# A gated linear attention and its perceptron on one core: the first pairs of step 0 by diagonal tiles, states inside their own outputs, and a new table of places

## The chip, the cores and the metric

One core of a Trainium2 chip runs the whole program. The metric is the device time in microseconds (us). Shorter is better. The core has five engines with a queue each: TensorE (PE, matrix products into the banks of PSUM), VectorE (DVE), ScalarE (ACT), GpSimd (POOL) and SyncE (SP, which issues the DMAs). Each works through its own queue in order and waits on semaphores for the others.

## The reference

Batch 4, 8 heads, 768 positions, 48 features a head; then a perceptron of width 2048 on 3072 tokens of 384.

```python
f = 1.0 / (1.0 + np.exp(-f_logit))
for t in range(S):
    state = f[:, :, t, :, None] * state + np.einsum('bhd,bhe->bhde', k[:, :, t], v[:, :, t])
    y[:, :, t] = np.einsum('bhd,bhde->bhe', q[:, :, t], state)
...
h = x @ w_in
g = np.where(pos, h, np.where(neg, 0.0, (h + beta) ** 2 / (4.0 * beta)))
return (g @ w_out).astype(np.float32)
```

## The kernel before

The 768 positions are six steps of 128. In a step the eight heads are four pairs; the program counts pairs through (0 to 3 are step 0, 4 to 7 step 1), and treats two pairs together. A step needs for each pair: the keys and queries multiplied by running products of the gates (`gate`, two scans by VectorE and two products), scores (keys by queries), a mask that keeps the past, the sums of masked scores by values, the products of the queries with the state from before, and the new state (keys turned over, by values). Scores in two halves of 64 positions are 64x64 tiles, of which four work at once in PE's array; the state after the first half, `later`, then serves the second half. The first step before does not use these tiles: `scores` makes whole 128x128 scores, each with a mask (`masks`), and `heads` and `thirds` make the sums.

The perceptron's work is 96 units (six steps of sixteen), and in each nine wide products into `ph` (line 317, `mm_in`) and nine into `po` (line 341, `mm_out`), of 512 columns. Between these groups stand the runs of the attention's small products for the step that comes next. Where they stand is a table: `TURNS` says behind which unit the keys of two pairs are turned over, `VISITS` gives four places for each two pairs: of their scores, of their states (`states_by_parts`), of the beginning of their outputs (`begin`), and of the end of their outputs (`outputs`). `START` lists the products of step 0 ahead of unit 0, and `AFTER` those behind it. When the places of the outputs' beginning and end are alike and nothing else is there, the outputs stand `alone` and borrow banks.

The order on each engine comes from a planner (`Plan`): it starts operations by a table of costs and writes out the order that results. It fills gaps of PE at the start with products of zeros (`warm`), and it has a model of how PE gets its instructions, in blocks of 256 (`BLOCK`, `FIRST_BLOCK`, `fetched`). Costs only set the order: on the chip every operation starts when its queue and its semaphores allow.

Constants (two masks and a unit matrix, `fixed`) are loaded. The values of the first two pairs (`va`) are loaded into `sd`.

Of the kernel before, what the change touches and what calls it, by code (L numbers as in the profile page):

```python
# [49 lines left out]
SMALL_PRODUCTS = ("scores", "scores_half", "heads", "thirds", "both", "begin", "before", "before_half", "part", "states", "parts", "parts_last")  # L50
# [4 lines left out]
            rows=316, turned_rows=150, scan=1140, dve=602, small=200, sums=467, gate=600, act=575, bits=660, round=485, copy=520, turned=412, sig=538, decay=226,  # L55
# [3 lines left out]
INSTRUCTIONS = dict(scores=32, scores_half=16, heads=32, thirds=32, both=128, begin=64, before=128, before_half=64, part=64, states=64, parts=128, parts_last=64, zeros=24, turn=8)  # L59
BLOCK, FIRST_BLOCK, AHEAD, BEHIND, FETCH, OFFSET, WAITS = 256, 193, 48, 40, 3700, 9, 1.0045  # L60
# [5 lines left out]
GATHER_BEHIND, GATHER_LATER = (0, 0, 0), 6000  # L66

TURNS = {4: 5.5, 6: 9.5, 8: 19.0, 10: 22.0, 12: 27.0, 14: 33.5, 16: 44.0, 18: 52.0, 20: 59.0, 22: 69.5}
VISITS = {4: (8.0, 8.0, 10.5, 10.5), 6: (10.5, 11, 13, 13), 8: (21.0, 21.0, 24.0, 24.0), 10: (24.0, 25, 29.0, 29.0), 12: (29.0, 32, 39.0, 39.0), 14: (39.0, 40.0, 42.0, 42.0), 16: (47.0, 47.0, 53.0, 53.0), 18: (53.0, 54.0, 60.0, 60.0), 20: (68.0, 68.0, 74.0, 74.0), 22: (74.0, 74.0, 77, 77)}
HOMES = [(k + 3) % 5 for k in range(25)]  # L70
START = (("scores", 0), ("mask", 0, 0), ("mask", 0, 1), ("last", 0), ("scores", 1), ("mask", 1, 0), ("mask", 1, 1), ("last", 1),
         ("scores", 2, 0), ("last", 2, 0), ("scores", 2, 1), ("last", 2, 1), ("first", 0), ("first", 1),
         ("mask", 2, 1), ("mask", 3, 1), ("mask", 2, 0), ("mask", 3, 0), ("second", 0), ("second", 1), ("second", 2), ("second", 3))
AFTER = {1.0: (('turn', 0), ('turn', 1), ('turn', 2)), 4.0: (('states', 0), ('states', 2)), 2.0: (('turn', 3),)}
# [24 lines left out]
class Plan:  # L99
# [7 lines left out]
    def add(self, engine, cost, emit, *deps, kb=0, count=None):  # L107
# [19 lines left out]
        if engine == "PE":  # L127
            o.count = count
# [7 lines left out]
    def fetched(self, o, zeros):  # L136
# [4 lines left out]
        self.able = max([self.able] + [d.end + d.lag(o) for d in o.deps if d.engine != "PE"])  # L141
        marks = [(b - AHEAD, 0, b) for b in self.blocks(last + AHEAD, end + AHEAD)]
        marks += [(b, 1, b) for b in self.blocks(last, end)] + [(b + BEHIND, 2, b) for b in self.blocks(last - BEHIND, end - BEHIND)]
        for at, kind, b in sorted(marks):
            t += (at - last) * step
            last = at
            if kind == 0:
                self.came[b + BLOCK] = t + FETCH
            elif kind == 1:
                t = max(t, self.came.get(b, 0))  # L150
            else:
                self.came[b + BLOCK] = max(self.came.get(b + BLOCK, 0), self.able + FETCH)
        self.at = end
        return t + (end - last) * step - o.start
# [5 lines left out]
    def order(self):  # L160
        index = {o: n for n, o in enumerate(self.ops)}
        self.at, self.came, self.able, idle = OFFSET, {}, 0, 0
# [15 lines left out]
        while done < len(self.ops):  # L178
# [31 lines left out]
            if e == "PE":  # L210
                o.zeros = zeros_for(o, idle)
                o.cost = self.fetched(o, o.zeros)
                idle = t + o.cost
# [17 lines left out]
def gla_moe(ctx: ExitStack, tc: tile.TileContext, ff, kqd, f0, vv, vad, vbd, wd, fixedd, gates, values, headsd, out):  # L231
# [26 lines left out]
    y3 = const.tile([R, 2, N], F32R, name="y3")  # L258
# [116 lines left out]
    set_kq = add("POOL", 1500, lambda: nc.gpsimd.memset(kq[NP - 1], 0.0))  # L375
# [7 lines left out]

    set_consts = add("POOL", 200, constants)

# [9 lines left out]
    add("PE", "zeros", lambda: warm(12), set_zeros)  # L395
# [108 lines left out]
    ready = {}  # L504
# [5 lines left out]
    def gate(m):  # L510
# [11 lines left out]
        if m == 0:  # L522
            ready["mask"] = ready["mask_t"] = ready["ident"] = dma(fixed, fixedd, 160)
            ready["f0"] = sca(200, lambda: nc.scalar.activation(f0s[:, 0:NI * NT * B], f0s[:, 0:NI * NT * B], AF.Sigmoid), dma(f0s, f0, 36))
        for h, (b0, b1) in enumerate(steps):
# [30 lines left out]
            for name, d in (("sg", sg), ("en", en), ("km", km), ("qm", qm), ("s2", s2)):  # L556
                c[name].append(d)
        to, f0m = whole(t), f0s[:, m * B:m * B + B]
# [4 lines left out]
    va = sd[:, 0:4 * B * 64].rearrange("u (b h e) -> u b h e", b=B, h=4)  # L563
# [13 lines left out]
    def elementwise(n):  # L577
# [14 lines left out]
        if p == NP - 1:  # L592

            cols = slice(0, 2 * N + B) if i else slice(0, N)
            gone = old(n - NP, "sc", "y", "tr", "db")
            c["to"] = []
            for t, m in enumerate(ours):
                o = gates_of[m]
                d = [o["km"], o["qm"], o["pf"][0]] if i else o["km"]
                o["to"] = [move(kq[NP - 1][z + 16 * SLICE[t]:z + 16 * SLICE[t] + 16, cols], kq[t][r:r + 16, cols], 64 if i else 32, d, set_kq, gone) for r, z in ((48, 0), (112, 64))]  # L600
# [18 lines left out]

    lent = {}  # L620
# [19 lines left out]
    def kn_of(n):  # L640

        return am[n] if n in (2, 3) else kn[n % 2]

    last_keys = [kn[0], kn[1], kn[0]]
    am_of = [am[0:2], am[2:4], [am[0], act_f[0][:, 0:N].rearrange("r (b c) -> r b c", b=B)], [am[1], kn[1]]]
# [24 lines left out]
    def masks(n, h):  # L670
# [5 lines left out]
        free = {(2, 0): lambda: att[0]["ys"][0], (3, 0): lambda: att[0]["ys"][1], (3, 1): lambda: att[3]["pt"][1]}.get((n, h), lambda: None)  # L676
        o = vec("dve", lambda: nc.vector.tensor_tensor(
            out=t, in0=ps, in1=mask.rearrange("u (o t) -> u o t", o=1).broadcast_to([C, B, C]), op=ALU.mult),
            c["sc"], ready["mask"], free())
# [10 lines left out]

    TILES = ((0, 0), (1, 1), (1, 0), (0, 1))
# [39 lines left out]
    def transpose_tensor(n, at=None):  # L731
# [9 lines left out]
        c["kn"] = [sca("turned", lambda: nc.scalar.copy(kn_of(n)[:, :, :R], ps[:, :, :R]), c["tr"], old(n - 2, "st") if n > 3 else [], [att[3]["sc"], att[3]["y"]])]  # L741
# [44 lines left out]
    def outputs(n, unit, alone):  # L786
# [5 lines left out]
        def decayed(which):  # L792

            def emit():
                parts = ((0, ds[n // 2 % 2]), (1, later))[::1 if which is False else -1]
# [16 lines left out]
        else:  # L812
            c["ys"] = add("PE", "before", decayed(None), need, c["yb"])
        y = add("PE", "part", attended(n, False, held, not alone), c["ys"])
# [10 lines left out]
        for h, t in enumerate((p, p + 1)):  # L825
            hi, lo = (y3[:, 0], y3[:, 1]) if t == NT else (xt[:, t, 0], xt[:, t, 1])
# [12 lines left out]
        if p > 0:  # L839

            moved[i] = [move(xt[r:r + 16, t].bitcast(F32), y3[z + 16 * SLICE[t]:z + 16 * SLICE[t] + 16].bitcast(F32), 64, x_of[i, NT], x_of[i, t])
# [61 lines left out]
    def heads(t, vs, a, deps, held=None):  # L903
# [3 lines left out]
        def emit():  # L907
            for m in range(B):
                for e in range(2):
                    nc.tensor.matmul(ps[64 * e:64 * e + 64, m], vs(m, e), a[e][:, m], start=t < 2 and m == 0, stop=False)  # L910
            if t == 2:
                close(ps)

        return add("PE", "heads", emit, deps, held)

    def thirds(t, a, deps):

        ps = firsts[t][1]
        k = 32 if SLICE[t] else 64

        def emit():
            for m in range(B):
                for e in range(2):
                    z = 192 + 128 * e + 32 * SLICE[t]
                    nc.tensor.matmul(ps[64 * e + 64 - k:64 * e + 64, m], vb[:, m, z - k:z], a[e][:, m], start=t == 2 and m == 0, stop=False)  # L925
            if t < 2:
                close(ps)

        return add("PE", "thirds", emit, deps)
# [134 lines left out]
    def of_first(t):  # L1064
# [236 lines left out]
```

## Time and profile before

| what | value |
|---|---|
| median of 3 runs | 468.5 us (467.7 to 468.75) |
| profiled execution | 467.89 us |
| its span, first to last instruction | 466.1 us |
| PE, DVE, ACT, POOL busy | 99%, 79%, 58%, 4% |
| granted TensorE clock | 1.0 of full speed |

A share of busy time says who works most, not who is waited for; the chain that ended last says that. In a chain a piece is one stretch of an engine's instructions, with its start and its length.

### The profile page before, as it was taken

What the parts mean: (1) busy time and instruction counts of PE and PEld (TensorE: products, weight loads), DVE (VectorE), ACT (ScalarE), POOL (GpSimd) and SP (SyncE); (2) the same over time, 40 slices, a digit from 0 to 9 for tenths busy, and PEclk for the clock granted to TensorE, in tenths of its full rate; (3) what the DMA queues carried; (4) which work ended last, traced back from release to release, by engine and by line L of the source; (5) the groups of instructions that cost most, each with busy time, mean ns of one, the idle gap of its engine ahead of it and who ended that gap; (6) DMA issues with size and microseconds to landing.
All of it is one profiled execution on the core that took longest, in us unless ns stands there. A gap on an engine that the chain in (4) does not pass through costs nothing.

```text
span 466.1 us, 10988 instructions
## 1 busy us (share of the span) xinstructions
PE 460.9 (99%) x4551; PEld 378.0 (81%) x4551; DVE 369.9 (79%) x712; ACT 268.0 (58%) x506; POOL 18.8 (4%) x67
## 2 busy tenths in 40 slices
PE   9999999999999999999999999999999999999996
PEld 4888888888888888888888888888888888888885
DVE  7999998998999998898989988685666755655633
ACT  4599999765655645555556446456445444544443
POOL 4100010000000000000000000000000000000000
PEclk9999999999999999999999999999999999999999
DMA  8889845172103152106413043045410334533101
GB/s 280 336 308 348 287 137 183 46 201 83 37 1 125 47 137 75 30 28 213 127 32 106 1 128 113 0 101 159 137 46 2 91 93 124 161 103 121 45 0 71
DMA packets 20307, 54.35 MB, mean 117 GB/s; under 512 B 3328, under 2 KB 3968, under 8 KB 20256
## 3 DMA queue, kind: packets, MB, share of 16 engines
q1 hardware_dynamic: 20256, 53.63, 36.2%
q8 instruction: 36, 0.59, 0.5%
q14 instruction: 15, 0.12, 0.1%
HBM read 44.77 MB, written 4.72 MB: 106 GB/s over the span
## 4 chain that ended last, share of the span: by engine, by line
PE 99%; DVE 0%; ACT 0%; issue 0%; DVEq 0%
PE po L341 43%; PE ph L317 42%; PE pa L773 2%; PE ph L392 2%; PE ph L712 2%; PE pa L804 2%; PE pa L877 1%; PE pa L738 1%; PE ph L664 1%; PE ph L953 0%; PE pa L712 0%; PE pa L925 0%; PE po L634 0%; PE ph L877 0%; PE pa L910 0%; PE pa L856 0%
## 5 line engine op out<-in xcount | busy, mean ns | idle before, releaser
L317 PE MATMUL ph<-x,w_hi 128*128 128x512 f32 x570 | 145.0, 390 | 0.0
L320 ACT ACTIVATE act<-ph,half 128x512 f32<-128x512 f32 x96 | 66.0, 688 | 103.7 <-PE ph L317 103.6
L317 PEld LDWEIGHTS ph<-x,w_hi 128*128 128x128 f32 x570 | 106.8, 188 | 22.2
L328 DVE SCALAR_TENSOR_TENSOR act<-ph,act 128x512 f32<-128x512 f32 x96 | 66.1, 689 | 42.4 <-ACT act L323 41.1
L331 ACT CAST ghi<-act 128x512 fp32r<-128x512 f32 x96 | 59.6, 621 | 60.3 <-DVE act L328 60.1
L341 PE MATMUL po<-ghi,w_hi 128*128 128x512 f32 x287 | 85.1, 398 | 0.0
L341 PE MATMUL po<-ghi,w_lo 128*128 128x512 f32 x287 | 82.7, 390 | 0.0
L341 PE MATMUL po<-glo,w_hi 128*128 128x512 f32 x287 | 82.6, 390 | 0.0
L334 DVE TENSOR_TENSOR glo<-act,ghi 128x512 fp32r<-128x512 f32 x96 | 66.2, 690 | 19.3 <-ACT ghi L331 16.8
L317 PE MATMUL ph<-x,w_lo 128*128 128x512 f32 x285 | 80.1, 389 | 0.0
L752 DVE STREAM_TRANSPOSE kn<-kq 32x128 f32<-32x128 f32 x224 | 67.7, 302 | 3.6
L341 PEld LDWEIGHTS po<-ghi,w_lo 128*128 128x128 f32 x287 | 53.9, 188 | 11.5
L341 PEld LDWEIGHTS po<-glo,w_hi 128*128 128x128 f32 x287 | 53.9, 188 | 11.4
L317 PEld LDWEIGHTS ph<-x,w_lo 128*128 128x128 f32 x285 | 53.5, 188 | 11.1
L323 ACT ACTIVATE act<-act 128x512 f32<-128x512 f32 x96 | 60.8, 634 | 2.5
L341 PEld LDWEIGHTS po<-ghi,w_hi 128*128 128x128 f32 x287 | 52.2, 188 | 11.1 <-ACT ghi L331 0.3
L465 DVE TENSOR_REDUCE ok<-raw 128x1 f32<-128x512 f32 x48 | 31.3, 680 | 13.1 <-DMA raw<-in_w 13.1
L542 DVE TENSOR_TENSOR_SCAN w<-f,least_w 128x512 f32<-128x512 f32 (+1 forms) x18 | 20.7, 1157 | 2.0 <-ACT f L538 2.0
L549 DVE TENSOR_TENSOR_SCAN f<-f,rec 128x512 f32<-128x512 f32 (+1 forms) x18 | 20.8, 1157 | 0.1
L546 POOL COPY end<-w 128x4 f32<-128x4 f32 (+1 forms) x20 | 5.6, 282 | 283.7 <-DVE w L542 283.5
L538 ACT ACTIVATE f<-f 128x513 f32<-128x513 f32 (+2 forms) x18 | 10.8, 608 | 10.0 <-DMA f<-in_f 9.7
L453 DVE TENSOR_TENSOR w_lo<-bits,w_hi 128x512 fp32r<-128x512 f32 (+1 forms) x25 | 16.2, 663 | 0.2
(134 smaller groups left out, 403.9 us busy)
## 6 DMA issues: line engine op xcount, KB each, us to landing
kq<-in_kq SPq DMA_DIRECT2D x18, 512.0 KB, 5.0
raw<-in_w SPq DMA_DIRECT2D x18, 512.0 KB, 3.5
raw<-in_w SPq DMA_DIRECT2D x14, 511.6 KB, 5.7
out_y<-raw SPq DMA_DIRECT2D x17, 256.0 KB, 2.3
f<-in_f SPq DMA_DIRECT2D x16, 256.5 KB, 3.3
v<-in_v SPq DMA_DIRECT2D x10, 384.0 KB, 4.8
raw_late<-in_w SPq DMA_DIRECT2D x7, 511.6 KB, 5.4
raw<-in_w SPq DMA_DIRECT2D x12, 256.0 KB, 4.3
```

Of the source, the lines that this page charges most:

```text
L317: nc.tensor.matmul(ps[:, to], w_in(w_hi if high else w_lo, j, kt), xt[:, kt, t, c], start=(n == 0), stop=(n == 8))
L320: nc.scalar.activation(a, ps, AF.Relu, bias=half, scale=0.5)
L323: nc.scalar.activation(a, a, AF.Square)
L328: nc.vector.scalar_tensor_tensor(out=a, in0=ps, scalar=1.0, in1=a, op0=ALU.max, op1=ALU.min)
L331: nc.scalar.copy(hi, a)
L334: nc.vector.tensor_tensor(out=lo, in0=a, in1=hi.bitcast(F32), op=ALU.subtract)
L341: nc.tensor.matmul(po[e][:, c], w_out(part, j, e), g[:, of], start=(j == 0 and n == 0 and c.start == 0), stop=(j == NJ - 1 and n == 2))
L453: l = vec(COST["dve"] * n // W, lambda: nc.vector.tensor_tensor(out=lo, in0=whole_val, in1=hi.bitcast(F32), op=ALU.subtract), h)
L465: seen.append(vec("dve", lambda z=z, op=op: nc.vector.tensor_reduce(out=ok[:, 1 + NG + z + c:2 + NG + z + c], in_=words_of(raw[2])[1].bitc ...
L542: s1 = vec(COST["scan"] if count == 1 else 602, lambda bwd=bwd, u0=u0, u1=u1: nc.vector.tensor_tensor_scan(out=wide(w[:, u0:u1]), data0=bw ...
L549: s2 = vec(COST["scan"] if count == 1 else 602, lambda fwd=fwd, b0=b0, b1=b1: nc.vector.tensor_tensor_scan(out=fwd, data0=fwd, data1=wide( ...
L752: nc.vector.transpose(kn[n % 2][u:u + 32, ::-1, r:r + 32], src[:, :, u:u + 32])
```

## The change

Step 0's first two pairs get the 64x64 tiles of the later steps. Their scores (`scores_of_first`) are 16 tiles a pair, then two masks in place of four (`masks_of_first`), then the sums in two parts (`sums_of_first`). The second part needs the state after the first half, so that state is made ahead of unit 0, in two products of 64 rows each (`states_of_first`): the first half goes to `later`, both halves together to the state. For that the keys of pairs 0 and 1 are turned over ahead of unit 0 as well, into a spare tile.

The masks and the unit matrix are no longer loaded: POOL makes them by selects. The values `va` now come into the tile of the last pair's keys and queries, so POOL clears that tile later, behind step 0's first outputs, and the copies between tiles that fill it come behind that. The small load for the decays of step 0 (`f0`) stands ahead of the second pair's keys in SP's queue. VectorE sets the zeros for PE after two other memsets, not before.

A place where states are made and outputs begin and end in one (`joint`) is new: the states by parts stand between the outputs' beginning and the rest, and the products on `later` come last. Places and planner numbers are new.

```diff
-TURNS = {4: 5.5, 6: 9.5, 8: 19.0, 10: 22.0, 12: 27.0, 14: 33.5, 16: 44.0, 18: 52.0, 20: 59.0, 22: 69.5}
-VISITS = {4: (8.0, 8.0, 10.5, 10.5), 6: (10.5, 11, 13, 13), ...
+TURNS = {4: 6.5, 6: 10.0, 8: 16.0, 10: 23.0, 12: 26.5, 14: 41.5, 16: 43.5, 18: 53.0, 20: 57.0, 22: 75.0}
+VISITS = {4: (7.0, 7.0, 10.5, 10.5), 6: (10.5, 12.5, 12.5, 12.5), ...
...
+START = (('turn', 0), ('last', 0, 0), ('last', 0, 1), ('both', 0, 0), ('both', 0, 1), ('turn', 1), ('both', 1), ('last', 1),
+         ('part', 1), ('mask_first', 0), ('scores', 2, 0), ('part', 0), ('scores', 2, 1), ('last', 2, 0), ('mask', 2, 0), ('mask_first', 1),
+         ('first', 0), ('last', 2, 1), ('mask', 3, 0), ('mask', 2, 1), ('mask', 3, 1), ('first', 1), ('slices', 0), ('head',),
+         ('slices', 1), ('slices', 2))
+AFTER = {0: (('turn', 2),), 3.5: (('turn', 3),), 5.5: (('states', 2),)}
...
-    set_kq = add("POOL", 1500, lambda: nc.gpsimd.memset(kq[NP - 1], 0.0))
+    def selected(t, op, base, slope, fill):
+        nc.gpsimd.affine_select(out=t, in_=t, compare_op=op, fill=fill, base=base, pattern=[[slope, t.shape[1]]], channel_multiplier=1)
...
+    def triangles():
+        nc.gpsimd.memset(fixed[:, 0:C + T], 1.0)
+        selected(mask, ALU.is_ge, 1 - C, 1, 0.0)
+        for k in range(2):
+            selected(mask_t[T * k:T * k + T], ALU.is_ge, 1 - T, 1, 0.0)
...
+    def states_of_first(l):
...
+                        nc.tensor.matmul(ps[r:z, a:a + D], kn_first[e][rows, m, r:z], va[rows, m, 2 * e + h, 0:D],
+                                         start=l == 1 and e == m == 0, stop=e == 1 and m == B - 1, skip_group_check=l == 0)
...
+        if l:
+            c["later"] = z = sca(412, lambda: nc.scalar.copy(later, ps[:R, 0:2 * B * D]), o)
...
         if alone:
             c["ys"] = add("PE", "before_half", decayed(True), need, [b[2] for b in held])
-        else:
+        elif not joint:
             c["ys"] = add("PE", "before", decayed(None), need, c["yb"])
-        y = add("PE", "part", attended(n, False, held, not alone), c["ys"])
+        y = add("PE", "part", attended(n, False, held, not alone), c["yb"] if joint else c["ys"])
+        if joint:
+            c["ys"] = add("PE", "before_half", decayed(None, slice(0, 1)), need[:2])
+            y = add("PE", "before_half", decayed(None, slice(1, 2)), need)
...
+        joint = [n for n in made if n in begun and n in ended and n not in new]
```

VectorE, at the end of step 0's gates. `kq_70` holds keys and queries of pair 2, `am`, `act` and `kn` the masked scores, `fixed` the masks, `bits` a piece of the weights. Before:

```order
L554 TENSOR_TENSOR kq_70<-kq_70,act_84 128x256
L677 TENSOR_TENSOR am_76<-pa_112,fixed 128x512
L677 TENSOR_TENSOR am_78<-po_117,fixed 128x512
L677 TENSOR_TENSOR am_77<-pa_113,fixed 128x512
L677 TENSOR_TENSOR am_79<-pa_114,fixed 128x512
L677 TENSOR_TENSOR act_83<-ph_116,fixed 128x512
```

After:

```order
L573 SCALAR_TENSOR_TENSOR act_84<-act_84,rec 128x256
L687 TENSOR_TENSOR am_76<-pa_112,fixed 128x512
L578 TENSOR_TENSOR kq_70<-kq_70,act_84 128x256
L687 TENSOR_TENSOR am_77<-pa_113,fixed 128x512
L473 SCALAR_TENSOR_TENSOR bits_95<-raw_late_102,bits_95 128x384
L780 TENSOR_TENSOR act_83<-ph_116,fixed 128x512
L780 TENSOR_TENSOR am_78<-po_119,fixed 128x512
```

The first pairs have two masks, not four, and one of them moved ahead of the last product of the gates.

PE, at the same place: scores of pair 2 (`po_119` and `ph_116`), the last pair's (`kn_80`), and what stands around them. Before:

```order
L634 MATMUL po_119<-kq_70 128x128
L634 MATMUL ph_116<-kq_70 128x128
...
L664 MATMUL ph_115<-kq_70,kn_80 128x128
L664 MATMUL po_118<-kq_70,kn_80 128x128
L910 MATMUL po_117<-am_76,sd 64x128
```

After (`y_87` are the turned keys, `kq_71` the values):

```order
L706 MATMUL pa_114<-kq_71,y_87 48x48 x16
L660 MATMUL po_119<-kq_70 128x128
L660 MATMUL ph_116<-kq_70 128x128
...
L761 MATMUL ph_115<-kq_70,kn_80 128x128
L761 MATMUL po_118<-kq_70,kn_80 128x128
L729 MATMUL pa_114<-am_77,kq_71 64x64
```

The half states came in among the scores, and the sums of the first pairs start with 64x64 tiles.

POOL, at the start of the program. Before:

```order
L368 MEMSET rec 128x512
L382 MEMSET half 128x1
L382 MEMSET up 128x1
L382 MEMSET down 128x1
L382 MEMSET top_of 128x1
L375 MEMSET kq_71 128x1028
L368 MEMSET sd 112x16
L546 COPY end_74<-w 128x2 x2
```

After:

```order
L373 MEMSET rec 128x512
L373 MEMSET fixed 128x128
L389 ISA
L389 AFFINE_SELECT fixed<-fixed 128x128
L396 MEMSET fixed 128x192
L389 AFFINE_SELECT fixed<-fixed 128x128
L389 AFFINE_SELECT fixed<-fixed 64x64 x2
```

Behind the rows shown the four small memsets, that of `sd` and the copies of `w` follow as before; the selects came in ahead of these copies, and the memset of the large tile went behind.

PE, in the run of states and outputs for pairs 6 and 7. Before, the parts stand alone between two wide groups:

```order
L317 MATMUL ph_116<-x_85,w_lo 128x512 x3
L877 MATMUL pa_114<-v,kn_80 48x48
L877 MATMUL ph_115<-v,kn_80 48x48 x2
...
L877 MATMUL pa_114<-v,kn_81 48x48
L341 MATMUL po_117<-ghi_88,w_hi 128x512
```

After, behind the 16 products of the outputs' beginning:

```order
L874 MATMUL pa_112<-am_78,v 48x64
L981 MATMUL pa_114<-v,kn_80 48x48
...
L981 MATMUL pa_114<-v,kn_81 48x48
L874 MATMUL pa_112<-am_78,v 48x64
...
L905 MATMUL pa_113<-kq_70,ds 48x64
L905 MATMUL pa_112<-kq_70,later 48x64
```

The parts moved from a run of their own into the run of the outputs, and 32 products stand between them and the first on `later`.

## Rows read from the trace of the kernel before

**Rows 1.** The page: busy time of PE, the chain that ended last, PE's instruction packets.

```profile
PE 460.9 (99%) x4551; PEld 378.0 (81%) x4551; DVE 369.9 (79%) x712; ACT 268.0 (58%) x506; POOL 18.8 (4%) x67
...
q8 instruction: 36, 0.59, 0.5%
...
PE 99%; DVE 0%; ACT 0%; issue 0%; DVEq 0%
```

**Rows 2.** The chain in order of time: start us, length us, piece.

```profile
23.17 2.18 PE ph L953 x9
...
27.40 1.15 PE pa L738 x12
...
32.69 0.39 PE pa L738 x4
...
41.25 1.57 PE pa L856 x64
42.83 2.27 PE po L341 x9
...
73.26 0.59 PE pa L773 x32
...
74.79 0.89 PE pa L804 x64
75.68 0.45 PE pa L773 x32
76.13 2.27 PE ph L317 x9
...
79.27 2.27 PE po L341 x9
81.53 2.04 PE ph L317 x9
```

**Rows 3.** Timeline of PE ahead of unit 0: start us, length us, instructions merged.

```profile
1.08 8.33 PE L392 MATMUL ph<-zeros 128*128 128x512 bf16 x27 [1.08 <-DVE zeros L365]
...
10.97 0.37 PE L664 MATMUL ph<-kq,kn 64*128 64x128 f32 x1
...
11.97 0.27 PE L634 MATMUL po<-kq 48*128 48x128 f32 x1
...
16.80 1.09 PE L910 MATMUL po<-am,sd 128*64 128x128 f32 x16
...
18.71 0.41 PE L925 MATMUL po<-act,v 128*32 128x128 f32 x2
```

**Rows 4.** Timeline of VectorE ahead of unit 0.

```profile
7.29 1.23 DVE L542 TENSOR_TENSOR_SCAN w<-f,least_w 128x512 f32<-128x512 f32 x1 [0.16 <-ACT f L538]
...
14.83 0.41 DVE L554 TENSOR_TENSOR kq<-kq,act 128x256 f32<-128x256 f32 x1
15.16 0.68 DVE L677 TENSOR_TENSOR am<-pa,fixed 128x512 f32<-128x512 f32 x1
```

**Rows 5.** Timeline of POOL ahead of unit 0.

```profile
1.41 0.95 POOL L375 MEMSET kq<- 128x1028 f32 x1
...
4.25 0.77 POOL L546 COPY end<-w 128x2 f32<-128x2 f32 x2 [1.84 <-DVE w L542]
...
9.69 1.13 POOL L559 TENSOR_TENSOR kq<-end,f0s 128x4 f32<-128x4 f32 x2 [0.81 <-ACT f0s L524]
```

**Rows 6.** Line 559 by itself: durations ns, first and last start us.

```profile
L559 POOLq MODIFY_POOL_CONFIG  x2: 6/6/6, 8.8 to 8.8; - x2
```

**Rows 7.** DMA queues from 12 to 20 us, then from 15 to 16 us.

```profile
q1 hardware_dynamic: 1075, 3.19, 99.2%
...
q8 instruction: 1, 0.02, 5.5%
```

**Rows 8.** Groups of instructions, shapes apart: the addition that makes `later`.

```profile
L881 DVE TENSOR_TENSOR later<-ph,ds 112x384 f32<-112x384 f32 x5 | 2.8, 555 | 0.8 <-PE ph L877 0.6 <-PE pa L877 0.2
```

More of the change, by code (lines that the diff above doesn't have):

```diff
@@ L47 @@
 NW = DM * DF // (128 * W)
-SMALL_PRODUCTS = ("scores", "scores_half", "heads", "thirds", "both", "begin", "before", "before_half", "part", "states", "parts", "parts_last")
+SMALL_PRODUCTS = ("scores", "scores_half", "both_half", "both_quarter", "states_half", "firsts", "heads", "thirds", "both", "begin", "before", "before_half", "part", "states", "parts", "parts_last")
 HOP, LANDING, PER_KB, LANES, FIRST, RISE = 200, 1350, 2.75, 8, 860, 700
@@ L56 @@
             issue=480, near=600, least=300)
-INSTRUCTIONS = dict(scores=32, scores_half=16, heads=32, thirds=32, both=128, begin=64, before=128, before_half=64, part=64, states=64, parts=128, parts_last=64, zeros=24, turn=8)
-BLOCK, FIRST_BLOCK, AHEAD, BEHIND, FETCH, OFFSET, WAITS = 256, 193, 48, 40, 3700, 9, 1.0045
+INSTRUCTIONS = dict(both_half=64, both_quarter=32, states_half=64, firsts=128, scores=32, scores_half=16, heads=32, thirds=32, both=128, begin=64, before=128, before_half=64, part=64, states=64, parts=128, parts_last=64, zeros=24, turn=8)
@@ L70 @@
 HOMES = [(k + 3) % 5 for k in range(25)]
[L71 to L74, printed above, removed]
+SELECTED = ()
@@ new lines, in sums_of_first, with emit @@
+    def sums_of_first(other):
+        c = att[0]
+        held = firsts[0:2]
+        def emit():
+            for m in range(B):
+                for e, k in TILES:
+                    h, half = 1 - k if other else k, slice(T * k, T * k + T)
+                    nc.tensor.matmul(held[h][1][64 * e:64 * e + 64, m, T * (1 - k):][:, :T], va[half, m, 2 * e + h], masked(0)[h][half, e * B + m],
+                                     start=other and m == 0, stop=other and m == B - 1, skip_group_check=not other)
+                for e, h in () if other else TILES:
+                    (r, z), a = HEADS[h], (e * B + m) * D
+                    nc.tensor.matmul(held[h][1][64 * e:64 * e + D, m, T:], later[r:z, a:a + D], query(e, e, m)[r:z, T:], start=False, stop=False, skip_group_check=True)
+        if other:
+            o = add("PE", "begin", emit, c["am"], c["lv"], [banks[h[0]] for h in held])
+            c["yb"] = sca("small", lambda: nc.scalar.copy(seen_y.rearrange("u (b c) -> u b c", b=B), held[0][1][0:1, :, T - 1:T + 1]), o)
+        else:
+            c["y"] = att[1]["y"] = add("PE", "firsts", emit, c["yb"], c["later"])
@@ L909, in emit, with slices_of_last @@
                 for e in range(2):
[L910 to L916, printed above, removed]
+                    nc.tensor.matmul(ps[64 * e:64 * e + 64, m], vb[:, m, 64 * e:64 * e + 64], am_of[2 + e][0][:, m], start=m == 0, stop=False)
+        att[2]["ys"] = add("PE", "heads", emit, [att[n]["am"][0] for n in (2, 3)], att[2]["lv"], banks[firsts[t][0]])
+    def slices_of_last(t):
         ps = firsts[t][1]
-        k = 32 if SLICE[t] else 64
         def emit():
```

174 lines of the change are left out of this document (109 added, 65 removed).

## The prediction

> **What bounds the kernel now.** I read the page first. TensorE (PE) is busy for 460.9 us of a span of 466.1, and the chain that ended last is PE for 99% of the span [rows 1]. So nothing counts unless it shortens PE's own queue or makes PE wait. Then I read the chain in order of time. From the first wide product of unit 0 at 23.17 us it is one unbroken queue: 192 groups of nine wide products (two per unit of the perceptron), 2.04 us each, and between them runs of small products (the attention's). A group behind such a run takes 2.27, so every run costs its own time plus 0.23 for the change of kind [rows 2]. The 192 groups make 391.7 us; the change doesn't touch them. Last I read the start. PE spends 8.33 us on 27 products of zeros and reaches real work at 9.4; the products of step 0 then run up to 23.17 [rows 2, 3]. In that stretch VectorE (DVE) is the one waited for: its last gate product starts at 14.83, then come eight masks of 0.68 each [rows 4]. The profiled execution took 467.89 us, 1.8 more than its span, and the median of the runs shown is 468.5, 0.6 more than that execution. I make the sum on 467.89 and add 0.6.
>
> **Part one, the runs between the groups.** Three items leave PE's queue behind unit 0.
>
> Transposes: before, 12 stand in one run of 1.15 and 4 in one of 0.39 [rows 2]. After, two runs of 4 are left; eight have moved ahead of unit 0. That is 1.54 less 0.78: -0.76.
>
> States of the first two pairs: the run at 41.25 takes 1.57 for two states products, plus 0.23 behind it [rows 2]. After, one of the two is left, 0.79 + 0.23: -0.78.
>
> Merged runs: states by parts stood alone in five runs, and in a sixth run behind outputs. One alone lasts from 76.13 + 2.27 = 78.40 to 79.27, so 0.87, and the group at 79.27 again takes 2.27 [rows 2]. After, four of them stand inside a run of their own outputs and two stand alone. The products are the same in number; the order before has 24 runs of small products behind unit 0, this one 21. Besides the transposes and states, three starts go: 3 x 0.23 = -0.69.
>
> Together -2.23.
>
> A merged run brings a new wait inside it: the products on `later` need VectorE's addition, which needs the parts just made. Between them PE has 16 products of the attention (0.45) and 16 on the older state (half of the 0.89 that 32 take) [rows 2]: 0.89 of cover. The addition takes 0.55 [rows 8], which leaves 0.34 for signals and for what VectorE has in hand, an operation of up to 0.68 [rows 4]. The order puts the addition right behind the second operation of a unit, which ends early in the run. I take 0.1 for all four; the bounds are 0 and 4 x 0.5 = 2.0. Nothing else in a run is longer: behind a wait there stand the rest of the run and the next group, so each is paid in full.
>
> **Part two, the start.** I follow PE's queue by hand. 23 zeros instead of 27, begun half a us later since VectorE fills two other tiles first, end near 9.0: by 8.33/27 each they would end at 8.7, but the early ones are the slow ones. Then, from the nearest rows: four transposes 0.39; eight products for the last pair 1.0 (10.97 to 11.97) [rows 3]; 16 diagonal tiles 0.47 (the 32 of a later pair fill the chain from 73.85 to 74.79); eight zeros 1.8; transposes 0.39; tiles 0.47; last pair 1.0; half a state 0.55 (between 0.4, half of a states product, and 0.87 for products on 64 rows); four scores 0.5; the copy that frees the bank 0.3; the other half state 0.55; four scores 0.5; four of the last pair 0.5. That reaches 17.4. VectorE can't hold this up: one mask now stands ahead of its last gate product, 14.83 + 0.41 + 0.65 = 15.9, while PE wants it at 16.4. Behind it are 16 + 32 products for the first pairs, 1.4 in place of the 1.91 between 16.80 and 18.71 [rows 3]; four products and a small copy 0.8; and the last pair's sums, which took 18.71 to 23.17 and now close one bank and not three, 4.2 [rows 2, 3]. Unit 0 would begin at 23.8 less the half us by which my roundings upward stack: 23.4, or +0.2. VectorE loses two masks here and nothing gains by it, as PE doesn't wait for it. The missing load of constants (160 KB) and the earlier small load for step 0's decays only move loads that PE meets later.
>
> **What the start newly asks for.** PE's instructions come in packets: 36 of 16 KB in all for 4551 matmuls with a weight load each, so some 250 instructions a packet [rows 1]. The planner's table counts them alike (193, then 256 each). Before, the first packet is seen between 15 and 16 us [rows 7], when PE has run about 230 instructions, and instruction 449 is reached only about 22.5. After, the early part is denser in instructions (each small product is four): I count 449 in the last pair's products at about 17.0. The packet is asked for when PE passes about 193, near 13 us after as before; so it should be there at 16 to 17. But all queues are full: the data queue holds the engines to 99% from 12 to 20 us [rows 7]. Bounds: no wait, or until the traffic ebbs at 20, 3.0. I take 0.7, near the lower end, since the row has a packet served amid that traffic. The next packet follows 3.6 us of PE work later, about its own delay, so I add none for it.
>
> The sum: -2.23 + 0.1 + 0.2 + 0.7 = -1.2, or 466.7 for the profiled execution, 467.3 in the median.
>
> **Weighed against the skill.** The Trainium skill (Runtime: NRT & Kernel Launch, section Instruction fetch mechanics) says that PE holds 2048 instructions, refilled in blocks of 16 KiB, and that crossing a block is mostly hidden. By that the 0.7 falls away. The trace agrees on the size of a block, but its 36 packets carry nearly the whole program while it runs, and one comes when PE has run no more than 230 instructions [rows 7], so it speaks for a far smaller store.
>
> **Rivals.**
>
> A: the instructions are there in time, as the packet at 15 to 16 [rows 7] would be. Groups and runs follow one another without a break in the chain before [rows 2], so no packet was late there; but none was asked of so early. -1.9: 466.6.
>
> B: the packet comes only as the loads end, at 20. PE stands for 3.0 at about 17: +1.1, 469.6. Against it: a packet passed in full traffic before.
>
> C, the one that ends slower: GpSimd (POOL) is late. It now makes the unit matrix and triangles by four selects, of a kind that the trace doesn't have, ahead of the two copies of 0.77 that free `w` [rows 5]; VectorE's scan at 7.29 [rows 4] waits for these copies, and behind it every gate. POOL starts on the selects near 1.5, so they have till 6.0, less 0.5 for memsets: 4.3 us with a margin. Nearest rows: a memset of 1028 columns 0.95, so 0.12 for 128; a first operation on four columns 0.56 (two in 1.13) [rows 5]. That makes about 2.5 for four, well inside. Beyond 4.3 VectorE is late by the excess; PE has 0.5 of slack there, and 1.2 with the wait for instructions. The gain is gone at an excess of 2.4, 6.7 us in all; at 8 us it is 469.8, slower. What decides is the loading of code ahead of the first select: before, the configuration at 8.8 [rows 6] is followed by an operation at 9.69 [rows 5], under 0.9.
>
> The Trainium skill (GPSIMD Engine Reference, section 2.1) gives about 6 us for the first call of a freshly loaded kernel. By that figure the four would take 7.7 us, and the time would be about 469.5; the 0.9 of the trace speaks against it.
>
> D: the merged runs only trade their starts for waits for `later`, 0.5 in each of four; the change then doesn't do what it says. -1.2 + 1.9 = +0.7: 469.2. For it: VectorE may have an operation of 0.68 in hand [rows 4], and 0.55 and that are more than the cover; against it: the addition's place in VectorE's order, behind work that ends early in the run.
>
> **How the numbers follow.** What a measurement can tell from no change is 0.2%, 0.9 us. Forecast 0.48 (its own range -0.5 to -1.9, 466.6 to 468.0), A 0.22, B 0.09, C 0.09, D 0.12. Faster by over 0.2%: two thirds of the forecast, nearly all of A and a rest: 0.56. Slower: most of C, half of B and a part of D: 0.13. Same: 0.31. The range runs from 465.7 (A, and half a state cheaper) to 469.2 (D, with B and C partly in it).
>
> **What will show it.** Right: 21 runs of small products; the group after a merged run at 2.27 and the run near 2.7 to 2.8; unit 0 at 23.4 to 24.4, with a gap of PE of up to 1 us in the last pair's products put on nothing but issue. Wrong: unit 0 later than 25 us; VectorE's third scan after 8 us, released by POOL; a gap ahead of the products on `later`. Most of all, the forecast fails if the start gives back the whole 2.2 us.

## The result: 0.58% slower

The changed kernel takes 470.94 us (median of 5 runs, 470.80 to 472.25); the kernel before, run beside it, 468.5 (467.7 to 469.19). The ratio is 1.0058, with a 95% interval of 1.0040 to 1.0077. That is 2.4 us more, where the prediction had 1.2 less, and above its range. The profiled execution took 470.95 us with a span of 469.2; before, 467.89 and 466.1. So 3.1 us are to be found between the two traces.

The page of the changed kernel, for [rows 1]: busy time, instruction packets (queue q8), and the chain that ended last.

```profile
PE 460.8 (98%) x4675; PEld 378.1 (81%) x4675; DVE 367.8 (78%) x702; ACT 268.0 (57%) x500; POOL 25.2 (5%) x73
...
q8 instruction: 37, 0.61, 0.5%
...
PE 88%; DMA 6%; DVE 3%; issue 1%; ACT 1%; DVEq 0%
```

PE is as busy as before (460.8 against 460.9) in a span that is 3.1 longer. So the 3 us are not more work: PE stands still for them, or has its work in another place. Besides, "issue" has a share of 1% in the chain: PE waits there for nothing that the profile names.

The chain at the start, for [rows 2, 3]: start us, length us, piece. L411 are the zero products, L706 the half states, L1026, L1014 and L1005 the last pair's sums, L346 the first products of a second operation.

```profile
2.42 7.07 PE ph L411 x22
9.50 0.39 PE pa L839 x4
...
11.60 1.83 PE ph L411 x8
...
15.53 0.85 PE pa L706 x32
...
21.32 1.00 PE po L1026 x16
22.32 1.02 PE pa L1014 x16
...
25.22 0.12 PE pa L1005
...
29.66 0.63 ACT ghi L336
...
30.33 0.73 PE po L346 x2
```

Unit 0 begins at 25.34; before, at 23.17 [rows 2]: 2.17 us later. From 9.50 to 25.34 PE is busy without a break, so it is PE's own queue that has grown. The first products of the second operation then start at 30.33, and the chain reaches them over ScalarE (`ghi`): PE waits there.

The chain in the runs between the groups, for [rows 2]: L874 is the sums of masked scores by values, L981 the states by parts, L905 the products on the older state and on `later`, L813 scores.

```profile
85.86 0.59 PE pa L874 x32
...
87.62 0.90 PE pa L905 x64
88.51 1.59 PE ph L322 x6
...
129.05 0.68 PE pa L905 x49
129.74 0.57 issue
130.31 0.38 PE pa L905 x12
...
378.33 0.88 PE pa L905 x55
379.21 1.02 issue
...
380.55 2.27 PE ph L322 x9
...
434.78 5.48 DMA raw<-in_w
...
441.63 0.96 PE po L346 x3
```

The reader is to see three things. A joint run (85.86 to 88.51) takes 2.65 us and shows no gap ahead of the products on `later`. And in two runs, at 129.74 and 379.21, PE stands in the middle of equal products for 0.57 and 1.02 us; the trace before has no such row anywhere behind unit 0. And near the end, at 441, PE waits for VectorE's `glo`, which in its queue is behind a reduction that waits for weights.

The trace records each instruction packet. Counting PE's instructions from 0 (a matmul and its weight load are two, every other row of its queue is one), both breaks stand at an exact place: PE resumes with instruction 3265 and 8641, which are 193 + 12 x 256 and 193 + 33 x 256. So the packets' ends are where the planner's table has them. This is how the two waits, and some of the experiments below, look in these records:

| kernel | PE passes the packet's end before | packet on the wire | PE goes on | wait | from landing to use |
|---|---|---|---|---|---|
| after | 127.69 | 127.95 to 128.89 | 130.31 | 0.57 | 1.42 |
| after | 376.88 | 377.53 to 378.83 | 380.23 | 1.02 | 1.40 |
| e1 | 17.80 | 20.45 to 21.39 | 22.81 | 0.70 | 1.42 |
| e2 | 75.88 | 77.26 to 78.14 | 79.62 | 1.28 | 1.48 |
| e2 | 230.97 | 232.70 to 233.66 | 235.05 | 2.18 | 1.39 |
| e4 | 376.26 | 377.08 to 378.04 | 379.42 | 0.85 | 1.38 |

In these six waits it takes 0.3 to 2.6 us from PE's passing the end of one packet until the next is on the wire, 0.9 to 1.3 on the wire, and 1.4 to 1.5 until PE uses it. Nine wide products (18 instructions) take 2.04 us, so among them 256 instructions last some 29 us; a full run has 384 instructions in 2.9 us, so two packets' ends can fall into one, and the time between them is then less than these delays.

But a packet isn't always so late: in after 14 of 37 are on the wire before PE reaches the end of the one before, by up to 4.5 us (one starts at 403.76, and PE is there at 408.27). All of these start while PE is among wide products, up to 40 instructions ahead of the end. So two ends in one run are not enough for a wait: over the twelve traces there are 19 places where PE passes two ends within 2.1 us and doesn't wait, and in each the first end stands 2 to 36 instructions behind the last wide product, and the packet is on the wire 1.1 to 4.5 us before PE is there (in before, at 161.37 and 163.19, the packet from 157.73). In the two breaks of after the first end stands 37 and 57 instructions behind it, and the packet comes 0.26 and 0.65 us after PE has passed. Of the packets that come late, the tightest in the trace before leaves 2.02 us from landing to use; after, three have 1.38 to 1.42. The third is a wait of 0.15 at 232.67, among wide products.

### The profile page after: what moved, and what is told of

Read it like the earlier page. It is cut to its first block, busy times and chain, and to the rows that moved or that the text cites. A ratio compares the mean times of both kernels' runs of the same rounds, so it can differ in the third digit from the quotient of the medians.

```text
span 469.2 us, 11225 instructions
## 1 busy us (share of the span) xinstructions
PE 460.8 (98%) x4675; PEld 378.1 (81%) x4675; DVE 367.8 (78%) x702; ACT 268.0 (57%) x500; POOL 25.2 (5%) x73
## 4 chain that ended last, share of the span: by engine, by line
PE 88%; DMA 6%; DVE 3%; issue 1%; ACT 1%; DVEq 0%
PE po L346 38%; PE ph L322 37%; DMA raw<-in_w 6%; PE pa L874 2%; PE pa L905 2%; PE ph L411 2%; DVE ok L490 2%; PE ph L813 2%; PE pa L981 1%; PE ph L761 1%; DVE act L333 1%; PE pa L839 0%; PE pa L813 0%; DVE glo L339 0%; PE pa L1026 0%
## 5 line engine op out<-in xcount | busy, mean ns | idle before, releaser
L346 PE MATMUL po<-ghi,w_hi 128*128 128x512 f32 x287 | 84.1, 395 | 0.3 <-ACT ghi L336 0.3
L346 PE MATMUL po<-glo,w_hi 128*128 128x512 f32 x287 | 82.6, 390 | 0.3 <-DVE glo L339 0.3
L346 PE MATMUL po<-ghi,w_lo 128*128 128x512 f32 x287 | 82.6, 390 | 0.0
L346 PEld LDWEIGHTS po<-glo,w_hi 128*128 128x128 f32 x287 | 53.8, 188 | 12.0 <-DVE glo L339 0.8
L346 PEld LDWEIGHTS po<-ghi,w_lo 128*128 128x128 f32 x287 | 53.9, 188 | 11.4
L346 PEld LDWEIGHTS po<-ghi,w_hi 128*128 128x128 f32 x287 | 52.9, 188 | 11.8 <-ACT ghi L336 0.8
L570 POOL COPY end<-w 128x4 f32<-128x4 f32 (+1 forms) x20 | 7.6, 380 | 275.3 <-DVE w L566 275.1
L477 ACT CAST w_hi<-bits 128x512 fp32r<-128x512 f32 (+1 forms) x25 | 14.4, 600 | 0.0
```

The lines of the kernel that those rows point to most:

```text
L346: nc.tensor.matmul(po[e][:, c], w_out(part, j, e), g[:, of], start=(j == 0 and n == 0 and c.start == 0), stop=(j == NJ - 1 and n == 2))
```

## The experiments

Times are medians beside runs of the kernel before on the same chip (468.35 to 468.82 in the four sets); ratios are against those.

**e1_no_zeros.** Is PE's queue what holds the start, and are the breaks tied to counts of instructions?

```diff
-            if o.engine == "PE" and o.zeros:
+            if o.engine == "PE" and o.zeros and o.start < 10000:
```

> The changed kernel without the eight zero products (16 instructions) that stand between the tile scores and the second transposes at 11.5 to 13.3 us. Theory (PE's own queue sets the start, since PE has no break from 13.27 to 25.34): unit 0 starts 1.5 to 1.8 us earlier, at 23.6 to 23.8. Rival (VectorE's gate products set it, the last at 15.56): unit 0 stays at 25.2 to 25.4. A second theory is told apart by the same run (the issue waits at 129.7 and 379.2 are waits for instruction packets, which lie at fixed counts of instructions): all that follows stands 16 instructions earlier in the packets, so both waits (0.57 and 1.02 us) go or move. Its rival (the waits belong to the runs of products in which they stand): both remain, shifted in time only. Both theories: 470.9 - 1.7 - 2.0 = 467.2 us; the first alone 469.2; the second alone 468.9; neither 470.9.

Measured: 470.31 us, ratio 1.0030 [1.0016, 1.0045]. The chain, with the last pair's sums and what PE waited for:

```profile
15.85 0.42 DVE kq L578
...
16.32 0.37 PE po L660
...
20.20 1.00 PE po L1026 x16
21.20 0.91 PE pa L1014 x13
22.11 0.70 issue
...
25.12 0.12 PE pa L1005
...
129.74 0.95 issue
```

The queue alone: 16 zero-product instructions less bring the last pair's sums from 21.32 to 20.20, 1.1 earlier; the rest of the 1.83 is lost on VectorE's last gate product (15.85 + 0.42), as the rival had it. But unit 0 comes only 0.1 earlier, for a third reason that neither theory had: at instruction 705 PE waits 0.70 us for a packet, and the 16 matmuls in which it waits take 2.05 us in all where they took 1.02. So the start has three bounds, one close behind the other. Of the breaks later on, that at 379 is gone, and that at 129.74 remains with 0.95: a shift of 16 instructions leaves the packet's end in the same run. Half of that expectation failed, since I took 16 instructions to be enough.

**e2_shift48.** The same work, 50 instructions more.

```diff
-                nc.tensor.matmul(opened["bank"], zeros, zeros.rearrange("p (o c) -> p o c", o=1).broadcast_to([128, 4, 128]),
-                                 start=opened["start"], stop=opened["start"])
+                opened["made"] = opened.get("made", 0) + 1
+                cuts = 2 if opened["made"] > 6 else 1
+                for z in range(0, 4, 4 // cuts):
+                    nc.tensor.matmul(opened["bank"][:, z * 128:(z + 4 // cuts) * 128], zeros, zeros.rearrange("p (o c) -> p o c", o=1).broadcast_to([128, 4 // cuts, 128]),
+                                     start=opened["start"], stop=opened["start"])
```

> The changed kernel with every zero product behind the first six cut into two of 256 columns: the same zeros, about 48 more instructions, nothing else. Theory (packets): from the places of the packets in the trace, a wait appears where a crossing then falls into a dense run: about 77, 210, 230, 276 and 379 us, 0.3 to 0.95 us each, and the one at 129.7 shrinks to 0.5 or goes; the time rises by about 2 us to 472 to 473. Rival (the waits belong to the runs): issue waits stay at 129.7 and 379.2 alone with 0.6 and 1.0 us, and the time stays at 470.9 within 0.4.

Measured: 479.23 us, ratio 1.0239 [1.0202, 1.0276]. Rows of its chain:

```profile
78.34 1.28 issue
212.14 1.40 issue
232.87 2.18 issue
281.42 1.49 issue
```

The places came as foretold (77, 210, 230, 276 and 379, each later by the waits ahead of it, so that the last, of 1.06, stands at 387.0), and there are two more, 0.74 at 20.7 and 1.05 at 299.7. The break at 129.7 is gone. Together they are 9.2 us. The rival is out: the work is the same, the places of the packets' ends have changed, and 8 us follow. That is about four times the 2 us that I gave, as I had counted one delay for all packets; here they begin 0.75 to 2.15 us after PE has passed the end before.

**e3_old_places and e4_before_places.** The two halves of the change apart: after with the two tables of before, and before with the two tables and the joint run of after. Of the four lines the first (`VISITS` goes with it in the same way, both ways as in the change's diff):

```diff
-TURNS = {4: 6.5, 6: 10.0, 8: 16.0, 10: 23.0, 12: 26.5, 14: 41.5, 16: 43.5, 18: 53.0, 20: 57.0, 22: 75.0}
+TURNS = {4: 5.5, 6: 9.5, 8: 19.0, 10: 22.0, 12: 27.0, 14: 33.5, 16: 44.0, 18: 52.0, 20: 59.0, 22: 69.5}
```

> The changed kernel with the two tables of places of before: the new start alone. If the start costs what the trace shows: unit 0 at 25.3, the wait ahead of the first down products 0.6 longer, the runs as before, so 467.9 + 2.2 + 0.6 - 0.8 (transposes) - 0.8 (states) = 469.1 us plus or minus waits for packets. If the start is paid back by the transposes and states that no longer stand in the units, as the prediction had it: 467.9 + 0.9 - 1.5 = 467.3 us or less.

> The kernel before with the two new tables and the joint runs, its own start: the places alone. The joint runs in the trace after are 2.65 us against 3.27 us for the two runs that they replace, three times: 1.9 us; two or three tenths more where a run was moved. Without a wait for packets 468.5 - 2 = 466.5 us. With waits like those of after (1.6 to 2.1 us) 468.5. If packets cause them, they stand at other places than the runs at 129.7 and 379.2 of after (the counts of instructions ahead of them differ); if the merged and full runs cause them, in the same runs.

Measured: the start alone 470.39 us, ratio 1.0037 [1.0021, 1.0052]; the places alone 469.94, ratio 1.0031 [1.0015, 1.0046]. Each half costs, and within their intervals the two make up the whole (0.37% and 0.31%, where the whole is 0.58%). The start alone has no break behind unit 0. It came out 1.3 us above my figure, and its profiled execution (470.07) 1.0; of this I find 0.2 at unit 0 (25.56 where after has 25.34), 0.4 in two zero products that stand among the transposes at 51 us, and 0.4 in small losses of PE from 111 us on. The places alone show the breaks in the same two runs, at other counts (3009 and 8385):

```profile
377.72 0.85 PE pa L804 x53
378.57 0.85 issue
```

By the test of the expectation, breaks in the same runs speak for the runs as their cause. But the counts are again packets' ends to the instruction (193 + 11 x 256 and 193 + 32 x 256), and e2 has the full run without its break, e1 the joint one, e6 both. So a break belongs to a dense run that reaches two packets' ends, the first of them too far in for its packet to come early, not to the run and not to a count as such. There is a third wait that the places bring in this kernel; its row in PE's timeline:

```profile
154.38 0.96 PE L341 MATMUL po<-ghi,w_hi 128*128 128x512 f32 x3 [0.26 <-ACT ghi L331]
```

**e5_turn_thrice.** What were the transposes behind unit 0 worth?

```diff
-            for m, (q, b) in enumerate(blocks(n)):
+            for m, (q, b) in (3 if n == 2 else 1) * list(enumerate(blocks(n))):
...
-                warm(o.zeros)
+                warm(o.zeros - 8 if o.start < 9500 else o.zeros)
```

> The changed kernel with the four transposes behind unit 0 emitted three times (the last write stands, the result is the same), twelve as in the kernel before; eight zero products fewer ahead of 9 us, where PE waits for keys anyhow, so that no later instruction changes its place in the packets. Theory (the transposes taken out of unit 0 stood in a wait that PE has anyway, 0.73 us ahead of the first down products): the run behind unit 0 grows from 0.75 to 1.5 us, the wait shrinks from 0.34 to nothing, the first down products start at 30.33 plus or minus 0.1, and the time stays at 470.9 plus or minus 0.3. Rival (they were on the path, as the prediction took them): first down products at 31.1, time 471.7.

Measured: 470.97 us, ratio 1.0051 [1.0036, 1.0067]; after has 470.94. PE's timeline of this kernel behind unit 0:

```profile
27.13 1.31 PE L839 MATMUL pa<-fixed,kq 112*128 112x112 f32 x12
...
30.37 0.84 PE L346 MATMUL po<-ghi,w_hi 128*128 128x512 f32 x3
```

The same of the changed kernel:

```profile
27.35 0.55 PE L839 MATMUL pa<-fixed,kq 112*128 112x112 f32 x4
...
30.33 0.96 PE L346 MATMUL po<-ghi,w_hi 128*128 128x512 f32 x3 [0.35 <-ACT ghi L336]
```

Eight transposes more (0.76) and the products on `ghi` start 0.04 later. Counted from unit 0, which came 0.2 earlier here, they cost 0.2. (The eight zeros left out did move the first transposes 1.6 earlier, since PE waits for no keys there; a wait of 0.70 for the packet at 705 and smaller delays took nearly all of that back.) The theory holds: the transposes stood in front of a wait that PE has anyway.

**e6_two_later.** Two runs moved, the rest of the change as it is.

```diff
-VISITS = {4: (7.0, 7.0, 10.5, 10.5), 6: (10.5, 12.5, 12.5, 12.5), 8: (20.0, 20.0, 21.5, 21.5), 10: (21.5, 25, 29.0, 29.0), 12: (29.0, 32.0, 39.0, 39.0), 14: (39.0, 43.0, 43.0, 43.0), 16: (51.0, 51.0, 53.0, 53.0), 18: (53.0, 56.0, 56.0, 56.0), 20: (66.0, 66.0, 75.0, 75.0), 22: (75.0, 75.5, 75.5, 75.5)}
+VISITS = {4: (7.0, 7.0, 10.5, 10.5), 6: (10.5, 12.5, 12.5, 12.5), 8: (20.0, 20.0, 22.0, 22.0), 10: (22.0, 25, 29.0, 29.0), 12: (29.0, 32.0, 39.0, 39.0), 14: (39.0, 43.0, 43.0, 43.0), 16: (51.0, 51.0, 53.0, 53.0), 18: (53.0, 56.0, 56.0, 56.0), 20: (66.0, 66.0, 75.0, 75.0), 22: (75.0, 77.0, 77.0, 77.0)}
```

> The changed kernel with two runs of products moved: tensor 10's full run half a unit later (place 22.0 for 21.5, the end of tensor 8 with it) and tensor 22's joint run from 75.5 to 77.0, with the same products in each. Theory (packets): in both runs the packet's end then lies ahead of the run, among the long products, so that only one falls into each: the issue waits at 129.7 (0.57) and 379.2 (1.02) go, and the joint run at the end takes 3.5 for 4.5 us; the time falls by 1.6 to 469.3. Rival (the waits come with the runs, or jump to another run): the two waits or others of their sum stay, 470.9 plus or minus 0.4.

Measured: 468.54 us, ratio 0.9999 [0.9987, 1.0011]. The two runs in its chain:

```profile
128.69 0.59 PE pa L874 x32
...
131.62 1.59 PE po L346 x6
...
380.96 0.59 PE pa L874 x32
...
383.62 2.27 PE po L346 x9
```

Both breaks are gone: the full run takes 2.93 for 3.69 us (127.50 to 131.19 in after), the joint one 2.66 for 3.98 (376.57 to 380.55), together 2.1 us, against 2.4 in the time. The profiled execution alone would flatter the move: in it unit 0 too comes 0.9 earlier than in after, for a reason of its own (last section), and some 0.3 is lost elsewhere. So the reading rests on the rows of the two runs and on the medians. The expectation had the mechanism not quite right: each run still holds two ends. But the first now stands 19 and 3 instructions behind the last wide product instead of 37 and 57, and its packet is on the wire 1.95 and 4.50 us before PE is there (128.73 and 380.90). With that the whole loss is gone. What is left of the change neither gains nor loses.

**e7_before_two_later.** The start of before with the places of e6: e4 with e6's line of `VISITS`.

> The kernel before, its own start, with the new places and joint runs, and the two runs moved as in e6. If the packets cost the new places what the traces show (0.62 and 0.85 us at 128.8 and 378.6 of e4): 469.9 - 1.5 = 468.4 us, under the kernel before by 0.4 us, and up to 0.6 more if VectorE's late gate at 153.5 (0.64) does not come again. If the places gain nothing beside their waits: 468.8. If other packets fall into runs: 469.9.

Measured: 469.86 us, ratio 1.0026 [1.0015, 1.0037]: the figure of the third case, but a packet is only a part of it. PE waits for one at 230 us:

```profile
229.95 0.80 issue
```

The last product of the second operation ends at 461.6, earlier than before (462.0) in spite of that, but the span at 468.6 instead of 466.1. SyncE's own waits at the end (us in total, times, the longest); the row that stands out:

```profile
SPq L1304 <- DVEq L1175: 2.9, 1, 2.9
```

VectorE's queue holds the end up for 2.9 us with no work in it.

**e8_narrow_zeros.** e6, its start shortened at the same count of instructions: the eight zero products between the tiles and the second transposes have 128 columns instead of 512.

```diff
-                warm(o.zeros)
+                warm(o.zeros, 1 if 9500 < o.start < 16000 else 4)
```

> The kernel of e6 with the eight zero products between the tile scores and the second transposes cut to 128 of their 512 columns: as many instructions as before, so that nothing changes its place in the packets, and 1.83 - 0.46 = 1.4 us less for PE. In e1 and e5 a start that was as much shorter met the packet that ends at instruction 705: PE stood 0.70 us for it and unit 0 came only 0.1 to 0.2 earlier. Theory (PE's queue and the packet behind it are close together, and the packet is asked for when PE crosses the one before, 1.4 us earlier here): unit 0 comes 0.4 to 0.9 earlier from the end of the first zeros than in e6 (15.75 us there), with an issue wait of 0.3 to 0.9 in the products on 128 rows at about 21.5; 468.0 us. Rival (PE's queue alone): no such wait, 1.4 earlier, 467.1. Rival (the data loads hold the packet as in e1): no gain, 468.5.

Measured: 468.10 us, ratio 1.0000 [0.9991, 1.0009]. Its chain:

```profile
11.96 0.55 PE ph L411 x8
...
21.97 0.52 issue
...
23.37 1.87 PE pa L1026 x32
```

The wait of 0.52 for the packet came where it was expected, and from the first transposes to unit 0 it is 15.5 us instead of 15.8 in e6. So only 0.3 comes back of the 1.3 by which PE's queue was cut. The time (0.4 under e6) is within what the two sets can tell.

**e9_before_padded and e10_before_padded_v.** The late end of e7: seven idle instructions more for ScalarE, then (shown) six for VectorE.

```diff
+    pad = const.tile([1, 8], F32, name="pad")
+    for k in range(6):
+        vec(60, lambda k=k: nc.vector.memset(pad[:, k:k + 1], 0.0), set_zeros).early = 1e6
```

> The kernel of e7 with seven more instructions for ScalarE at its start (sigmoids of one number, that nothing reads). In e7 the last product ended at 461.5, as early as in the kernel before (461.8), yet PE's last wait took 3.84 us in place of about 1.0, and one more instruction packet of another engine's queue came at 468.2, behind the end. Theory (one engine's program crosses a packet's end just at its last instructions; ScalarE's has 578 there against 581 to 590 in the others): with seven more the late packet goes, the end takes 4.4 us behind the last product instead of 7.2, and the time falls by 2.6 to 467.2. Rival (it isn't ScalarE's, or not a packet's): 469.9.

> The kernel of e7 with six more instructions for VectorE near its start (a memset of one number each, that nothing reads); PE's program is the same word for word. e9 showed that the late end isn't ScalarE's: it stayed. At the end of e7 VectorE's branch is over at 463.98 and its next instruction, a semaphore, comes at 467.57, while the other engines go on within 0.1; SyncE waits for it from 464.70 to 467.62. Theory (VectorE's program, 696 rows there against 695 and 697 in kernels without this end, crosses a packet's end just behind its branch): with six more the 3.6 us go to 0.1 to 0.6, the end behind the last product takes 4.4 for 7.2 us, and the time is 469.9 - 2.8 = 467.1, up to 0.8 more where a packet at 230 is late as in e7: under the kernel before by 0.5 to 1.3. Rival (the count doesn't matter, the branch itself is slow): 469.9.

Measured: with ScalarE's seven, 470.00 us, ratio 1.0041 [1.0028, 1.0054]: nothing won, my first guess at the engine was wrong. With VectorE's six, 467.50 us, ratio 0.9976 [0.9963, 0.9989]. SyncE's waits at the end of that kernel:

```profile
SPq L1178 <- SPq L1178: 0.9, 3, 0.5
SPq L1307 <- PEq L1307: 0.6, 2, 0.5
```

There is no row for VectorE among them any more, and nothing else was changed: six instructions that do nothing make the program 2.4 us faster, so the count matters and the branch alone isn't slow. That they move VectorE's last ones off a packet's end is the theory, and not shown: in e7 the last packets on record ahead of 467.57, where VectorE goes on, land at 465.15 and 465.83. This version, with the start of before, the new places and joint runs, two of them moved, beats both kernels: the one before by 0.24%, with an interval of 0.11% to 0.37%.

## Why the prediction was wrong

Its sum was -1.2 on 467.89; measured were +3.06 (470.95). Step by step, what a run costs being counted from the end of one group of nine wide products to the end of the next, less the 2.04 of the group itself:

- **Part two, the start: the step that failed first, by size.** Forecast +0.2, measured +2.17. The prediction's order of PE's queue was right, and that nothing interrupts it. Its pieces were too small: on 32 or 64 rows a half state takes 0.85 (0.55 forecast, and there are two), 16 diagonal tiles (32 matmuls) 0.62 (0.47), four scores 0.64 (0.5), eight products of the last pair 1.09 (1.0). Each piece of another kind begins with some 0.2 that a row from the middle of a long run doesn't show. That makes 1.1, after taking off a copy's 0.3 that PE doesn't wait for. Another 0.5 I had subtracted as "roundings upward", of which there were none. And the zeros end at 9.5, not 9.0. That may be luck: they become twice as fast at 6.9 us here and at 5.75 in the trace before (last section), worth some 0.6, an estimate from their two rates. Unit 0 at 25.34 is beyond the 25 that the prediction named as its failure.
- **What the start newly asks for: the right mechanism in the wrong place.** The packet that I priced at +0.7 landed at 15.88, and instruction 449 was reached at 18.59, so PE didn't wait. Where packets did hold PE, it put the cost at nothing, and this is the second step that failed, as large as the first: "no packet was late there", it says of the runs before, and carries that over to the new places. In the runs they cost 0.8 + 1.3 = 2.1 us (e6). Rows of before show that there was no wait; they don't show by how much it was missed, and 2.02 us from landing to use against the 1.3 to 1.5 that PE needs was a margin of only half a us.
- **Transposes: forecast -0.76, measured about -0.1** (1.49 for 1.61 behind the first groups; e5: the eight are worth 0.2 at most). They were PE's cover for the chain `act`, `ghi` of the first unit. I took the run at 27.40 [rows 2] as path since PE was busy in it, and didn't look at what PE would wait for without it.
- **States of the first pairs: forecast -0.78, measured -0.7** (1.08 us for 1.80). Right.
- **Merged runs: forecast -0.69 + 0.1, measured -1.1.** Right in kind. A states run alone costs 1.09 and an outputs run 2.18, a joint one without a wait 2.89: 0.38 each for three, where I counted one start of 0.23. There is no wait on `later` in the rows.
- **Not forecast:** 0.6 at 441 us, where VectorE's operation `glo` stands behind a reduction that waits for the last weights. e1 and e4 don't have it, e5 and e6 do; I didn't look for its cause. And 0.35 at 232.8, in part the third wait for a packet, against 0.19 that the kernel before loses at 288.

With the measured terms: 2.17 + 2.1 - 0.1 - 0.7 - 1.1 + 0.6 + 0.2 = +3.2, against 3.06: no term of size is missing.

The rivals: A had the packet of the start in time, which it was, and yet missed the time, since the start itself was mis-sized. B (PE stands at 449 until 20 us) fell. C (GpSimd's selects late) fell by these rows of its timeline and VectorE's scan:

```profile
1.62 0.29 POOL L389 TENSOR_SCALAR_AFFINE_SELECT fixed<-fixed 128x128 f32<-128x128 f32 x1
...
2.18 0.78 POOL L389 TENSOR_SCALAR_AFFINE_SELECT fixed<-fixed 128x128 f32<-128x128 f32 x3
...
7.63 1.22 DVE L566 TENSOR_TENSOR_SCAN w<-f,least_w 128x512 f32<-128x512 f32 x1
```

The selects are over at 2.96, and the scan begins at 7.63, not behind 8. The 6 us that the Trainium skill (GPSIMD Engine Reference, section 2.1) gives for a first call aren't seen. D (waits on `later`) fell as told. Its sign was right by accident: the joint runs did cost what they save, but for packets.

On the packets: PE goes on 1.3 to 1.5 us after a landing in all 19 waits of 0.5 us and more that I counted over eight runs. The Trainium skill (Runtime: NRT & Kernel Launch, section Instruction fetch mechanics) has the crossing of a block mostly hidden. In long products it is nearly so (0.15 us at 232.67); in runs of 64-row products that reach a second end it isn't (0.57 and 1.02 us), and here the 2.1 us that this costs made the loss.

Of e2 to e10, the comparison that carries most is e6 against after: the same products, two runs moved by 9 and 27 wide products, and 2.4 us. That the packets made the loss is shown by it and by e2. That the start takes back what the places and joint runs gain is shown by e3, by e10, which has the places without it, and by the chain; what a better order of that start would give was not tried beyond e1 and e8.

## What to carry to other kernels

Where a tensor engine's program is unrolled, count its instructions: find the packets' ends (here 193 + 256 n), and look at each stretch in which 256 small instructions run in under some 3 to 4 us (an estimate from the delays of the table). Where two ends fall into one, move it so that the first stands at its very beginning, behind long products: within 20 instructions there was no wait in 18 of 19 such places here, and at the other, in e2, a further end stands only 4.1 us earlier. Before a piece of work is called a gain because it leaves a busy queue, look at what the next instruction would wait for without it. And price many small pieces each with its own beginning, not by the rate inside a long run of them.

## What was not expected of the hardware

- **Six instructions, 2.4 us.** The end of e7 (2.9 us of SyncE waiting for VectorE) came with 704 instructions of VectorE's on the page; with 710 it was gone, and before and after, with 712 and 702, don't have it. That VectorE has packets' ends too, and one of them right behind the branch at the end, would explain it; no record shows it.
- **The zeros at the start are not of fixed length.** 22 equal products of zeros took 7.28 us in after, 6.40 in e6, 7.50 in e3. In the trace each starts 0.427 us after the last at first, and 0.216 from some moment on, which is twice as fast, as between the two levels of 1.2 and 2.4 GHz; that moment is 5.2 us in e6, 6.9 in after and 7.3 in e3, though PE had done the same until then. The granted clock of the windows, first of after and then of e6, reads 1.00 in this stretch all the same; it is the count of products that tells:

```profile
5.00:6.00 1.00, 1.00 (x3) 0.30 (x2) 0.79 (x2) 0.00 (x0) 0.00 (x0) 1.00 1.50 285
```

```profile
5.00:6.00 1.00, 1.00 (x5) 0.40 (x4) 1.00 (x4) 0.00 (x0) 0.06 (x1) 1.00 1.14 286
```

Since real work is queued behind the zeros, unit 0 moves with them: in e6 it comes 0.9 earlier than in after, in e3 0.2 later, each time 15.8 us behind the start of the first transposes. The twelve executions of e6 lie between 467.5 and 469.8. What sets the moment stays open.
